# Memory attention and gated FFN on one core: tokens in five padded chunks, the first batch's keys loaded first, one summing group a batch

## The chip, the cores and the metric

The kernel runs on 1 core of a Trainium2 chip. The metric is the device time of one execution in microseconds (us). Three runs of the kernel before took 730.93 to 731.76 us, median 731.49.

## What is computed

```python
# q, k, v: (8, 8, 576, 64); phi: (8, 8, 576, 32); w_in: (512, 2048); w_out: (2048, 512); float32
a = softmax(phi, axis=2)                    # over the 576 tokens, for each memory
k_m = einsum('bhsm,bhsd->bhmd', a, k)       # 32 memory keys a head
v_m = einsum('bhsm,bhsd->bhmd', a, v)
attn = softmax(q @ k_m.T / 8, axis=-1)      # over the 32 memories
x = (attn @ v_m) laid out as (8 * 576, 512)
h = x @ w_in
out = (h * erf(log1p(exp(-abs(h))) + maximum(h, 0))) @ w_out
```

## The kernel before

The 8 batches follow each other. For each batch the kernel first makes the memories, folds the values into the first weight (vw = v_m times w_in, head by head), makes the attention weights `at`, and then runs the FFN in 16 steps k of 128 hidden columns: `ffn1` (L666) gives h for 576 tokens in two halves of 288, ACT and DVE make g out of it, and `ffn2` (L758) adds g times w_out to four PSUM tiles `pso` of 128 tokens each. The 64 tokens that are left over from 4 x 128 are collected in `rest`, two batches side by side, and multiplied later (`ffn2_rest`, `psr`). Float32 operands are mostly split into a high and a low float32r part, so that a product is three matmuls (hi hi, hi lo, lo hi); the first four FFN1 steps and the first sixteen FFN2 steps run in plain float32 ("exact"), because the splits aren't ready then.

The weights come as 64-bit words. `decode` (L423) turns one piece of 256 columns into float32: two ACT steps (L435, L439) and three DVE steps (L429, L443, L465). The first batch needs w_in piece by piece: `vw` for piece c, then FFN1 of steps 2c and 2c + 1.

The memories of a batch: `memories` (L485) loads phi twice. `phiT` has memories on partitions: there DVE takes the maximum over tokens, and ACT makes the exponential whose sum is the softmax's divisor (`prs`). `phi` has tokens on partitions, in four chunks of 128 rows and a last one of 64 (L393 to L402, two transfers); the maximum is turned to that layout with ACT (L495) and TensorE (L501), DVE adds it and ACT takes exp (L507 to L516). `one_memory` (L530) then sums keys and values of four heads over the tokens:

```python
for c, (s0, ln) in enumerate(SC):
    for j in range(4):
        h = 4 * g + j
        nc.tensor.matmul(
            out=get(ps)[M * j : M * (j + 1), 0, :],
            lhsT=get(a)[:ln, c, h * M : (h + 1) * M],
            rhs=get(("kv", b, h // 2))[:ln, c, :, h % 2, :],
```

Keys and values of a head stand side by side (128 columns), four heads write the four quarters of the partitions, and there are two such groups (g = 0, 1) a batch: 20 matmuls each, shown as 40 in the profile, since a float32 matmul is recorded as two. ACT scales the sums (L550, L552), TensorE turns them (L557), ACT copies them to `km` and `vm` (L570, L573). `attention` (L616) makes scores of q and km for one half of a batch's tokens (u = 2b and 2b + 1) and runs their softmax on DVE and ACT (L629 to L650).

The order on every engine is written by a planner when the kernel is built (`Plan.order`, L126 on): each operation has costs, a rank and reads and writes, buffers of a pool are taken in turn, and the planner gives each engine a fixed order. In the start it also puts filler matmuls (`fill`, L361: zeros times zeros, "idle") into gaps that it foresees on TensorE, so many as fit. The engines run their queues in order; all loads and stores are issued by SP in one queue.

Of the kernel before, what the change touches and what calls it, by code (L numbers as in the profile page):

```python
# [28 lines left out]
SCRATCH = 1024  # L29

# [39 lines left out]
class Plan:  # L70
# [5 lines left out]
    SWITCH = 92.0  # L76
    RELOAD = 100.0
# [160 lines left out]
def tile_memory_attention_then_erf_softplus_ffn(  # L238
# [13 lines left out]
    H = 2 * kv.shape[1]  # L252
# [13 lines left out]
    SC = [(c * P, min(P, S - c * P)) for c in range((S + P - 1) // P)]  # L266
    RAW = 4
# [10 lines left out]
        for n, b, kw in (  # L278
# [9 lines left out]
            ("ot", 2, {}),  # L288
# [6 lines left out]
    room.update({"g_hi": 3, "g_lo": 3, "raw": RAW, "ot": 2, "ps": 4, "sc": 2, "dk": 1, "phiT": 2})  # L295
    room.update({f"pso{d}": 1 for d in range(NT)})
    for n in ("pmx", "psm", "prs"):
# [10 lines left out]
        "ot": ("ot", [P, DM], F32),  # L308
# [18 lines left out]
    def mm(n, exact):  # L327
        return 2 * (2 * n / 2.4 + 2.5) if exact else n / 2.4 + 11.7
# [10 lines left out]
    zeros = const.tile([P, 512], BF16, name="zeros")  # L339
# [21 lines left out]
    def fill(n):  # L361
        if n and not idle:
            idle.append(pools["po"].tile([P, DM], F32, name="idle", tag="pso0"))
        for _ in range(n):
            nc.tensor.matmul(out=idle[0], lhsT=zeros[:, :P], rhs=zeros, start=True, stop=True)


    def load(rank, key, nbytes, emit):
        op(SP, 60, rank, [], [key], emit, nbytes=nbytes)

    def load_weight(rank, name, c):
# [14 lines left out]
        load(rank, key, P * 8192, emit)  # L386

    def load_phiT(rank, b, g):
        key = tile_("phiT", "phiT", b, g)
        load(rank, key, P * S * 4,  # L390
             lambda: nc.sync.dma_start(out=get(key), in_=phiT[b, g * P : (g + 1) * P, :]))

    def load_tokens(rank, key, src, n_bytes, view):  # L393
        n = S // P
        load(rank, (key, "whole"), S // P * P * n_bytes, lambda: nc.sync.dma_start(
            out=view()[:, :n], in_=src[: n * P].rearrange("(p c) e -> p c e", c=n)))
        load(rank + 0.001, (key, "last"), SC[-1][1] * n_bytes, lambda: nc.sync.dma_start(
            out=view()[: SC[-1][1], n], in_=src[n * P :]))

    def load_phi(rank, b):  # L400
        key = tile_("raw", "phi", b, shape=[P, len(SC), H * M], pool="raw")
        load_tokens(rank, key, phi[b], H * M * 4, lambda: get(key))  # L402

    def load_kv(rank, b, p, tag="raw"):
        key = tile_(tag, "kv", b, p, shape=[P, len(SC), 2, 2, D], pool=tag)
        load_tokens(rank, key, kv[b, p], 4 * D * 4,
                    lambda: get(key).rearrange("p c x h d -> p c (x h d)"))

    def load_q(rank, u, tag="raw"):
        key = tile_(tag, "q", u, shape=[P, NP_, U], pool=tag)  # L410
        b, hf = divmod(u, 2)
        load(rank, key, P * NP_ * U * 4, lambda: nc.sync.dma_start(
            out=get(key),
            in_=qT[b, :, hf * U : (hf + 1) * U].rearrange("(p r) s -> r p s", r=P)))
# [70 lines left out]
    def memories(rank, rank_2, b):  # L485
        a = ("phi", b)
        n, ln = S // P, SC[-1][1]
        bias = tile_("dk", "bias", b, shape=[P, NG, P], pool="att")
        for g in range(NG):
# [5 lines left out]
            op(ACT, 320, rank, [mx], [(bias, g)], lambda g=g, mx=mx: nc.scalar.activation(  # L495
                get(bias)[:, g], ident, AF.Identity, scale=0.0, bias=get(mx)))
        ps = tile_("ps", "psa", "max", b, shape=[P, H * M], pool="ps")

        def turn():
            for g in range(NG):  # L500
                nc.tensor.transpose(  # L501
                    out=get(ps)[:, g * P : (g + 1) * P], in_=get(bias)[:, g], identity=ident
                )

        op(PE, 2 * 108, rank, [bias], [ps], turn)
        op(DVE, on_dve(n * H * M), rank, [(a, "whole"), ps], [(a, "whole")],
           lambda: nc.vector.tensor_tensor(  # L507
               out=get(a)[:, :n], in0=get(a)[:, :n],
               in1=get(ps).unsqueeze(1).to_broadcast([P, n, H * M]), op=ALU.add))
        op(DVE, on_dve(H * M), rank, [(a, "last"), ps], [(a, "last")],  # L510
           lambda: nc.vector.tensor_tensor(
               out=get(a)[:ln, n], in0=get(a)[:ln, n], in1=get(ps)[:ln], op=ALU.add))
        op(ACT, on_act(n * H * M), rank, [(a, "whole")], [(a, "whole")],
           lambda: nc.scalar.activation(get(a)[:, :n], get(a)[:, :n], AF.Exp), kind="exp")
        op(ACT, on_act(H * M), rank, [(a, "last")], [(a, "last")],
           lambda: nc.scalar.activation(get(a)[:ln, n], get(a)[:ln, n], AF.Exp), kind="exp")  # L516
# [10 lines left out]
        for g in range(NG):  # L527
            one_memory(rank_2 + g * 0.01, b, g)

    def one_memory(rank, b, g):  # L530
        a, rs = ("phi", b), ("prs", b, g)
        ps = tile_("ps", "psa", "kmvm", b, g, shape=[P, 4, P], pool="ps")
        t = tile_("dk", "kvk", b, g, shape=[P, 3 * D], pool="att")
        ps_2 = tile_("ps", "psa", "turn", b, g, shape=[P, 4, P], pool="ps")

        def sums():
            for c, (s0, ln) in enumerate(SC):
                for j in range(4):
                    h = 4 * g + j
                    nc.tensor.matmul(  # L540
                        out=get(ps)[M * j : M * (j + 1), 0, :],
                        lhsT=get(a)[:ln, c, h * M : (h + 1) * M],
                        rhs=get(("kv", b, h // 2))[:ln, c, :, h % 2, :],
                        start=(c == 0),
                        stop=(c == len(SC) - 1),
                    )

        op(PE, len(SC) * 215, rank, [a] + [("kv", b, 2 * g + j) for j in range(2)], [ps], sums,
           kind="small", holds=[t])
        op(ACT, 300, rank, [ps, rs], [(t, 0)], lambda: nc.scalar.activation(  # L550
            get(t)[:, 0 : 2 * D], get(ps)[:, 0, :], AF.Identity, scale=get(rs)))
        op(ACT, 190, rank, [(t, 0)], [(t, 1)], lambda: nc.scalar.activation(  # L552
            get(t)[:, 2 * D : 3 * D], get(t)[:, 0:D], AF.Identity))

        def turn():
            for r in range(2):
                nc.tensor.transpose(  # L557
                    out=get(ps_2)[:, r, :], in_=get(t)[:, r * D : (r + 2) * D], identity=ident
                )

        op(PE, 2 * 108, rank, [t], [ps_2], turn)
        for par in range(2):
            rows = slice(par * D, (par + 1) * D)

            def view(which, rows=rows, par=par):
                v = get(ps_2).rearrange("p r (pr e m) -> p r pr e m", e=2, m=M)
                return v[rows, which, :, par, :]

            op(ACT, 145, rank, [ps_2], [(("km", b % 2), (g, par))],
               lambda rows=rows, par=par, view=view: nc.scalar.activation(  # L570
                   km[b % 2][rows, 2 * g : 2 * g + 2], view(par), AF.Identity, scale=SCALE))
# [375 lines left out]
```

## Time and profile before

| | before |
|---|---|
| median of three runs | 731.49 us (730.93 to 731.76) |
| the profiled execution | 729.75 us, of which the span from first to last instruction is 728.0 us |
| TensorE matmuls (PE) | 720.0 us busy, 99% of the span, 4816 recorded |
| VectorE (DVE) | 521.0 us, 72% |
| ScalarE (ACT) | 449.9 us, 62% |
| GpSimd (POOL) | 98.7 us, 14% |
| bytes moved | 64.75 MB, mean 89 GB/s |

The profile shows one execution. Its busy share of PE holds the filler matmuls, and matmuls overlap, so that the busy share alone doesn't tell where time can be gained; the timeline of PE does. In the rows a line number is that of the kernel, `out<-in` are the program's names, `x40` counts the instructions that a row merges, and a row of a timeline begins with start and length in us.

### The profile page before, as it was taken

How to read it: one execution, taken by the hardware profiler on the slowest of the kernel's cores; microseconds unless marked ns; L12 is line 12 of the kernel's file. 1: busy time of each engine (PE TensorE's matmuls, PEld its weight loads, DVE VectorE, ACT ScalarE, POOL GpSimd, SP SyncE). 2: the span in 40 equal slices, each digit the busy share in tenths (PEclk: the TensorE clock that was granted, in tenths of full speed). 3: DMA queues.
4: the chain of work that ended last, by engine and by line, in shares of the span. 5: the costliest groups of instructions: out<-in, count | busy, mean ns of one | idle time of the engine just before them, and what ended most of it. 6: DMA issues, size and time to landing. Idle time of an engine off the chain costs nothing.

```text
span 728.0 us, 12307 instructions
## 1 busy us (share of the span) xinstructions
PE 720.0 (99%) x4816; PEld 553.8 (76%) x4816; DVE 521.0 (72%) x963; ACT 449.9 (62%) x708; POOL 98.7 (14%) x246
## 2 busy tenths in 40 slices
PE   9999999999999999999999999999999999999997
PEld 4456555578887888888788887888878788888885
DVE  3899999689677685877755587777854587666631
ACT  5799999875747666594644556474754266454611
POOL 0011001120111111111111011111111111111110
PEclk9999999999999999999999999999999999999999
DMA  9996332421503115111310214211210100010002
GB/s 321 391 389 227 100 149 82 161 100 43 173 24 108 42 39 178 35 59 34 107 57 1 91 48 127 70 59 33 66 33 1 59 15 0 1 45 15 1 1 72
DMA packets 30393, 64.75 MB, mean 89 GB/s; under 512 B 2688, under 2 KB 13440, under 8 KB 29312
## 3 DMA queue, kind: packets, MB, share of 16 engines
q1 hardware_dynamic: 30336, 63.97, 26.1%
q8 instruction: 38, 0.62, 0.4%
q14 instruction: 19, 0.16, 0.1%
HBM read 54.53 MB, written 9.44 MB: 88 GB/s over the span
## 4 chain that ended last, share of the span: by engine, by line
PE 87%; DMA 6%; ACT 4%; DVE 1%; SPq 1%; issue 1%
PE pso L754 48%; PE psh L681 26%; PE psr L754 6%; PE psa L583 5%; DMA w<-w_in 4%; PE psa L540 2%; DMA kv<-kv 2%; ACT w L439 1%; ACT w L435 1%; ACT e L709 0%; ACT L709 0%; PE psa L557 0%; ACT e L704 0%; DVE w L443 0%; ACT vw_hi L354 0%
## 5 line engine op out<-in xcount | busy, mean ns | idle before, releaser
L754 PE MATMUL pso<-wo,g_hi 128*128 128x512 f32 x896 | 280.8, 395 | 0.0
L704 ACT ACTIVATE e<-h 128x576 f32<-128x576 f32 x128 | 88.0, 687 | 171.5 <-DVE h L696 170.9
L754 PEld LDWEIGHTS pso<-wo,g_hi 128*128 128x128 f32 x896 | 160.0, 188 | 31.8 <-issue 6.3
L754 PE MATMUL pso<-wo,g_lo 128*128 128x512 f32 x448 | 176.1, 393 | 0.0
L696 DVE COPY h<-psh 128x288 f32<-128x288 f32 x239 | 107.8, 452 | 42.8 <-PE psh L681 41.2
L681 PE MATMUL psh<-at_hi,vw_hi 128*128 128x288 f32 x496 | 113.7, 310 | 0.0
L681 PE MATMUL psh<-at_hi,vw_lo 128*128 128x288 f32 x496 | 106.0, 295 | 0.3 <-DVE vw_lo L356 0.3
L681 PE MATMUL psh<-at_lo,vw_hi 128*128 128x288 f32 x496 | 106.1, 295 | 0.0
L681 PEld LDWEIGHTS psh<-at_hi,vw_hi 128*128 128x128 f32 x496 | 84.5, 188 | 27.8 <-issue 8.2
L735 POOL CAST rest<-g_hi 128x64 fp32r<-128x64 f32 x112 | 51.1, 457 | 391.3 <-DVE g_hi L730 385.5
L728 DVE TENSOR_TENSOR e<-e,h 128x576 f32<-128x576 f32 x112 | 82.7, 751 | 26.5 <-ACT e L709 26.4
L754 PEld LDWEIGHTS pso<-wo,g_lo 128*128 128x128 f32 x448 | 84.1, 188 | 19.2
L730 DVE CAST g_hi<-e 128x576 fp32r<-128x576 f32 x112 | 50.7, 457 | 63.1 <-PE pso L754 51.1
L731 DVE TENSOR_TENSOR g_lo<-e,g_hi 128x576 fp32r<-128x576 f32 x112 | 86.3, 771 | 4.4
L709 ACT ACTIVATE e<-e 128x576 f32<-128x576 f32 x128 | 80.3, 675 | 0.4
L681 PEld LDWEIGHTS psh<-at_hi,vw_lo 128*128 128x128 f32 x496 | 79.8, 188 | 0.7 <-DVE vw_lo L356 0.5
L681 PEld LDWEIGHTS psh<-at_lo,vw_hi 128*128 128x128 f32 x496 | 79.1, 188 | 0.0
L735 POOL CAST rest<-g_lo 128x64 fp32r<-128x64 f32 x112 | 37.8, 338 | 110.8 <-DVE g_lo L731 103.7
L754 PE MATMUL pso<-w,g 128*128 128x512 f32 x112 | 52.5, 599 | 0.0
L754 PE MATMUL psr<-wo,rest 128*128 128x512 f32 x192 | 49.0, 390 | 0.0
L354 ACT ACTIVATE vw_hi<-psa 128x512 fp32r<-128x512 f32 (+1 forms) x68 | 34.9, 556 | 19.6 <-PE psa L583 19.5
L356 DVE TENSOR_TENSOR vw_lo<-psa,vw_hi 128x512 fp32r<-128x512 f32 (+1 forms) x68 | 42.0, 632 | 6.5 <-ACT vw_hi L354 6.3
(82 smaller groups left out, 716.0 us busy)
## 6 DMA issues: line engine op xcount, KB each, us to landing
kv<-kv SPq DMA_DIRECT2D x32, 512.0 KB, 4.2
q<-qT SPq DMA_DIRECT2D x16, 576.0 KB, 5.0
w<-w_in SPq DMA_DIRECT2D x8, 1024.0 KB, 11.6
w<-w_out SPq DMA_DIRECT2D x8, 1024.0 KB, 11.2
out<-ot SPq DMA_DIRECT2D x32, 256.0 KB, 2.0
phiT<-phiT SPq DMA_DIRECT2D x16, 288.0 KB, 2.9
phi<-phi SPq DMA_DIRECT2D x8, 512.0 KB, 5.7
kv<-kv SPq DMA_DIRECT2D x32, 64.0 KB, 4.2
```

The costliest lines, as they stand in the source:

```text
L354: lambda: nc.scalar.activation(get_hi(), get_src(), AF.Identity))
L356: lambda: nc.vector.tensor_tensor(out=get_lo(), in0=get_src(), in1=get_hi().bitcast(F32), op=ALU.subtract))
L583: nc.tensor.matmul(out=get(ps[par])[p * M : (p + 1) * M, :], lhsT=w()[rows, p, :], rhs=x()[rows, p, :], start=True, stop=True,)
L681: nc.tensor.matmul(out=get(ps), lhsT=x[:, g, k % 4 * P : (k % 4 + 1) * P], rhs=y[:, g, :], start=(n + g == 0), stop=(n == len(parts) - 1 a ...
L696: lambda: nc.vector.tensor_copy(out=keep(), in_=get(ps)),
L704: last[:] = [op(ACT, on_act(S), rank, [("h", i)], [e], lambda: nc.scalar.activation(get(e), get(("h", i)), AF.Softplus), kind="softplus", ...
L709: last[:] = [op(ACT, on_act(S), rank, [e], [e], lambda: nc.scalar.activation(get(e), get(e), AF.Erf), kind="erf", edge=edge, after=last)]
L728: op(DVE, on_dve(S), rank, [e, h], [e], lambda: nc.vector.tensor_tensor(out=get(e), in0=get(e), in1=get(h), op=ALU.mult))
L730: op(DVE, on_dve(S, 1), rank, [e], [hi], lambda: nc.vector.tensor_copy(out=get(hi), in_=get(e)))
L731: op(DVE, on_dve(S), rank, [e, hi], [lo], lambda: nc.vector.tensor_tensor(out=get(lo), in0=get(e), in1=get(hi).bitcast(F32), op=ALU.subtract))
L735: lambda x=x, y=y: nc.gpsimd.tensor_copy(out=rest[:, k, x, cols], in_=get(y)[:, NT * P :]))
L754: nc.tensor.matmul(out=o, lhsT=y, rhs=z, start=(start and n == 0), stop=(stop and n == len(parts) - 1))
```

## The change

- **Tokens in five chunks on padded partitions.** The host lays keys, values and phi out as five chunks of 116 rows (the last 112), each on 128 partitions with zeros behind. phi, and each of the four kv tiles, is one transfer of 640 KB (before 512 + 64 KB). No chunk has 64 rows or fewer.
- **Keys and values apart.** A kv tile holds keys or values of four heads, not both of two; a summing matmul has 64 columns and not 128.
- **The first batch.** Its `phi` isn't loaded. The exponentials of `phiT` are turned on TensorE in ten transposes and copied out of PSUM (`numbers_of`), four chunks at once on ACT and the last on DVE. The sums of all keys are one group, those of all values another. The transfers stand in another order (`FIRST`).
- **The other batches** have one summing group with all four kv tiles (80 matmuls), four transposes in one piece, and half as many copies to km and vm, each twice as wide. Batch 1's loads and memories are due four steps later (`o - 8`, not `o - 12`).
- **Rest.** In the first 16 steps POOL writes the high and the low part of the left-over columns itself; `rest_split` on ACT and DVE is gone.
- **Stores.** The pool `ot` is gone; a store's tile takes a buffer of `phiT`. The last batch's tiles are copied out by ACT alone, not half by DVE.
- `raw` has five buffers, not four; the planner's costs of changing between small and large matmuls, and of a wide float32r matmul, are raised a little; a filler reads 128 zeros four times, and not 512.

```diff
-    FIRST = ["phiT0", "phiT1", "phi", "kv0", "kv1", "in0", "kv2", "kv3", "q0", "q1", "in1", "out0"]
+    FIRST = ["phiT0", "phiT1", "k0", "k1", "q0", "in0", "v0", "v1", "q1", "in1", "out0"]
...
+    def load_kv(rank, b, x, g):
+        key = tile_("raw", "kv", b, x, g, shape=[P, NC, 4 * D], pool="raw")
+        load(rank, P * NC * 4 * D * 4, [key],
+             lambda: nc.sync.dma_start(out=get(key), in_=kv[b, x, g]))
...
+        if not b:
+            tile_("raw", *a, shape=[P, NC, H * M], pool="raw")
+            n = NC - 1
+            for g in range(NG):
+                numbers_of(rank, b, g, range(n), tile_("ps", "psa", "a", g, shape=[P, n, P], pool="ps"), 0)
+            last = tile_("ps", "psa", "a", NG, shape=[P, NG, P], pool="ps")
+            for g in range(NG):
+                numbers_of(rank, b, g, range(n, NC), last, g)
+        for turn_n, part in enumerate(parts):
+            one_memory(rank_2 + turn_n * 0.01, b, part)
+
+    def numbers_of(rank, b, g, cs, ps, at):
...
+        def turn():
+            for c in cs:
+                nc.tensor.transpose(
+                    out=get(ps)[:ln, at + c - cs[0], :], in_=get(t)[:, c * ROW : c * ROW + ln], identity=ident
+                )
...
         def sums():
-            for c, (s0, ln) in enumerate(SC):
-                for j in range(4):
-                    h = 4 * g + j
-                    nc.tensor.matmul(
-                        out=get(ps)[M * j : M * (j + 1), 0, :],
-                        lhsT=get(a)[:ln, c, h * M : (h + 1) * M],
-                        rhs=get(("kv", b, h // 2))[:ln, c, :, h % 2, :],
-                        start=(c == 0),
-                        stop=(c == len(SC) - 1),
-                    )
...
+            for n, g in enumerate(gs):
+                for y, x in enumerate(xs):
+                    for c, ln in enumerate(ROWS):
+                        for j in range(4):
+                            h = 4 * g + j
+                            nc.tensor.matmul(
+                                out=get(ps)[M * j : M * (j + 1), n, y * D : (y + 1) * D],
+                                lhsT=get(a)[:ln, c, h * M : (h + 1) * M],
+                                rhs=get(("kv", b, x, g))[:ln, c, j * D : (j + 1) * D],
+                                start=(c == 0),
+                                stop=(c == NC - 1),
+                            )
...
+            op(POOL, 400, rank, [t], part[:1], lambda: nc.gpsimd.tensor_copy(
+                out=rest[:, k, 0, cols], in_=get(t)[:, NT * P :]))
+            op(POOL, 400, rank, [t, part[0]], part[1:], lambda: nc.gpsimd.tensor_tensor(
+                out=rest[:, k, 1, cols], in0=get(t)[:, NT * P :],
+                in1=rest[:, k, 0, cols].bitcast(F32), op=ALU.subtract))
...
-        t = tile_("h" if final else "ot", "ot", *o)
-        halves = [(0, DM // 2, ACT), (DM // 2, DM, DVE)] if final else [(0, DM, ACT)]
...
+        t = tile_("h" if final else "phiT", "ot", *o)
+        op(ACT, on_act(DM, True), rank - 30, [o], [t],
+           lambda: nc.scalar.activation(get(t)[:, :DM], get(o), AF.Identity))
```

Since the planner orders the work, the diff doesn't show how instructions move. The first place is SP's queue at the start of the program. Before:

```order
L391 DMA phiT<-phiT 128x576 x2
L395 DMA phi<-phi 128x1024
L397 DMA phi<-phi 64x256
L395 DMA kv<-kv 128x1024
L397 DMA kv<-kv 64x256
...
L377 DMA w<-w_in 128x4x256
...
L412 DMA q<-qT 128x4x288 x2
L377 DMA w<-w_in 128x4x256
```

Now:

```order
L396 DMA phiT<-phiT 128x576 x2
L405 DMA kv<-kv 128x1280 x2
L410 DMA q<-qT 128x4x288
L382 DMA w<-w_in 128x4x256
L405 DMA kv<-kv 128x1280 x2
L410 DMA q<-qT 128x4x288
L382 DMA w<-w_in 128x4x256
L387 DMA w<-w_out 128x1024
```

The keys and one q now stand ahead of the first piece of w_in, and the values behind it; before, two of four kv pieces (left out above) stood behind it, and both q behind them.

The second place is PE's queue at the memories of a later batch, among FFN matmuls (`pso`, `psh`); `w_in, vm` is a vw block (the numbers are those of buffers), `kv, phi` the sums, `ident, kvk` the transposes of the sums. Before:

```order
L583 MATMUL psa<-w_in_103,vm_102 32x512 x8
L540 MATMUL psa<-kv,phi 32x128 x20
L681 MATMUL psh<-at_hi,vw_hi 128x288 x2
...
L557 MATMUL psa<-ident,kvk 128x128 x2
L754 MATMUL pso<-wo,g_hi 128x512 x2
L754 MATMUL pso<-wo,g_lo 128x512
L540 MATMUL psa<-kv,phi 32x128 x20
L754 MATMUL pso<-wo,g_hi 128x512 x2
```

Now:

```order
L617 MATMUL psa<-w_in_100,vm_99 32x512 x8
L566 MATMUL psa<-kv,phi 32x64 x80
L715 MATMUL psh<-at_hi,vw_hi 128x288 x2
...
L587 MATMUL psa<-ident,kvk 128x128 x4
L774 MATMUL pso<-wo,g_hi 128x512 x2
```

Two groups of 20, one of them alone among FFN matmuls, have become one of 80 behind a vw block. In batches 1 to 7 there were 14 such groups, 8 of them alone; now there are 7, one alone. The whole program has 78 fillers, and had 112.

## Rows read from the trace of the kernel before

**Rows 1.** The page, part 1: busy us (share of the span) xinstructions of each engine.
```profile
PE 720.0 (99%) x4816; PEld 553.8 (76%) x4816; DVE 521.0 (72%) x963; ACT 449.9 (62%) x708; POOL 98.7 (14%) x246
```

**Rows 2.** Windows: stretch, its length, each engine's busy us, PEclk, DMA share, GB/s.
```profile
0.00:48.70 48.70, 46.52 (x346) 23.62 (x347) 34.96 (x60) 34.14 (x62) 1.80 (x7) 1.00 1.00 363
48.70:130.00 81.30, 80.12 (x556) 46.63 (x554) 75.54 (x123) 78.06 (x126) 8.41 (x16) 1.00 0.46 158
```

**Rows 3.** Timeline of PE, 0 to 60 us; in brackets idle before it and releaser.
```profile
15.43 1.97 PE L540 MATMUL psa<-kv,phi 128*32 128x128 f32 x40
...
22.09 7.73 PE L365 MATMUL idle<-zeros 128*128 128x512 bf16 x35
29.66 4.04 PE L681 MATMUL psh<-at,vw_hi 128*128 128x288 f32 x16
...
38.08 0.66 PE L583 MATMUL psa<-w_in,vm 64*32 64x256 f32 x16
...
48.76 1.88 PE L754 MATMUL pso<-w,g 128*128 128x512 f32 x4
```

**Rows 4.** Chain of waits, 0 to 60 us: start, us, what.
```profile
14.30 13.64 DMA w<-w_in
...
28.01 10.14 DMA w<-w_in
```

**Rows 5.** Timeline of PE, pieces between 231 and 282 us.
```profile
231.56 0.71 PE L583 MATMUL psa<-q,km 64*32 64x288 f32 x16
232.20 0.73 PE L754 MATMUL pso<-wo,g_hi 128*128 128x512 f32 x2
...
270.18 1.09 PE L583 MATMUL psa<-w_in,vm 64*32 64x512 f32 x16
271.20 1.43 PE L540 MATMUL psa<-kv,phi 128*32 128x128 f32 x40
...
279.29 0.40 PE L754 MATMUL pso<-wo,g_lo 128*128 128x512 f32 x1
279.62 1.43 PE L540 MATMUL psa<-kv,phi 128*32 128x128 f32 x40
280.98 0.73 PE L754 MATMUL pso<-wo,g_hi 128*128 128x512 f32 x2
281.55 0.40 PE L754 MATMUL pso<-wo,g_lo 128*128 128x512 f32 x1
281.79 0.63 PE L754 MATMUL pso<-wo,g_hi 128*128 128x512 f32 x2
```

**Rows 6.** Line 540 (count: ns min/median/max, first and last start); windows of its instructions.
```profile
L540 PEld LDWEIGHTS psa<-kv,phi x640: 102/110/110, 9.6 to 529.0; 128*32 128x32 f32 x128, 64*32 64x32 f32 x32
L540 PE MATMUL psa<-kv,phi x640: 269/273/297, 9.6 to 529.1; 128*32 128x128 f32 x128, 64*32 64x128 f32 x32
279.62:279.65 0.03, 0.03 (x4) 0.03 (x5) 1.00 0.00 0
```

**Rows 7.** Waits of PE's weight loads, 120 to 140 us: total, times, longest.
```profile
PEld psa L540 <- DMA kv<-kv: 0.8, 1, 0.8
```

**Rows 8.** Timelines of ACT and DVE, 0 to 70 us.
```profile
5.59 0.76 ACT L521 ACTIVATE phiT<-phiT,pmx 128x576 f32<-128x576 f32 x1
...
13.00 1.16 ACT L435 ACTIVATE w<-w 128x1024 int32<-128x1024 uint32 x1
...
15.20 1.23 DVE L443 SCALAR_TENSOR_TENSOR w<-w 128x1024 int32<-128x1024 int32 x1 [1.68 <-ACT w L439]
...
21.87 1.37 DVE L632 TENSOR_REDUCE smx<-sc 128x18 f32<-128x576 f32 x2
```

**Rows 9.** Timelines of the last copies; last row: groups by form, busy us, mean ns.
```profile
723.37 0.42 DVE L803 COPY ot<-psr 128x256 f32<-128x256 f32 x1 [0.94 <-PE psr L754]
...
723.83 0.38 ACT L800 ACTIVATE ot<-psr 128x256 f32<-128x256 f32 x1 [0.98 <-DVE ot L803]
...
L800 ACT ACTIVATE ot<-psr 128x512 f32<-128x512 f32 x3 | 1.7, 581 | 0.0
```

More of the change, by code (lines that the diff above doesn't have):

```diff
@@ L265, in tile_memory_attention_then_erf_softplus_ffn @@
     REST = S - NT * P
-    SC = [(c * P, min(P, S - c * P)) for c in range((S + P - 1) // P)]
-    RAW = 4
+    NC = phi.shape[2]
+    ROWS = [min(ROW, S - c * ROW) for c in range(NC)]
+    assert NC == -(-S // ROW) and D < ROWS[-1]
+    RAW = 5
     HB, EB = 5, 5
@@ L364, in fill, with load @@
         for _ in range(n):
-            nc.tensor.matmul(out=idle[0], lhsT=zeros[:, :P], rhs=zeros, start=True, stop=True)
-    def load(rank, key, nbytes, emit):
-        op(SP, 60, rank, [], [key], emit, nbytes=nbytes)
+            nc.tensor.matmul(
+                out=idle[0].rearrange("p (n c) -> p n c", c=P), lhsT=zeros,
+                rhs=zeros.unsqueeze(1).to_broadcast([P, DM // P, P]), start=True, stop=True,
+            )
+    def load(rank, nbytes, keys, emit):
+        op(SP, 60, rank, [], keys, emit, nbytes=nbytes)
     def load_weight(rank, name, c):
@@ L384, in emit @@
                 )
-        load(rank, key, P * 8192, emit)
+        load(rank, P * 8192, [key], emit)
     def load_phiT(rank, b, g):
         key = tile_("phiT", "phiT", b, g)
-        load(rank, key, P * S * 4,
+        load(rank, P * S * 4, [key],
              lambda: nc.sync.dma_start(out=get(key), in_=phiT[b, g * P : (g + 1) * P, :]))
[L393 to L398, printed above, removed]
-    def load_phi(rank, b):
[L401 to L407, printed above, removed]
+    def load_phi(rank, b):
+        key = tile_("raw", "phi", b, shape=[P, NC, H * M], pool="raw")
+        load(rank, P * NC * H * M * 4, [key], lambda: nc.sync.dma_start(out=get(key), in_=phi[b]))
+    def load_kv(rank, b, x, g):
+        key = tile_("raw", "kv", b, x, g, shape=[P, NC, 4 * D], pool="raw")
+        load(rank, P * NC * 4 * D * 4, [key],
+             lambda: nc.sync.dma_start(out=get(key), in_=kv[b, x, g]))
     def load_q(rank, u, tag="raw"):
@@ L494, in memories @@
                 out=get(mx), in0=get(mx), scalar1=-1.0))
[L495 to L499, printed above, removed]
+        if b:
+            bias = tile_("dk", "bias", b, shape=[P, NG, P], pool="att")
             for g in range(NG):
-                nc.tensor.transpose(
-                    out=get(ps)[:, g * P : (g + 1) * P], in_=get(bias)[:, g], identity=ident
-                )
@@ L505, in memories @@
[L505 to L516, printed above, removed]
+                op(ACT, 320, rank, [("pmx", b, g)], [(bias, g)], lambda g=g: nc.scalar.activation(
+                    get(bias)[:, g], ident, AF.Identity, scale=0.0, bias=get(("pmx", b, g))))
@@ L517, in memories @@
+            op(ACT, on_act(NC * H * M), rank, [a], [a], lambda: nc.scalar.activation(
+                get(a)[:ROW], get(a)[:ROW], AF.Exp), kind="exp")
         for g in range(NG):
@@ new lines, in numbers_of, with turn, keep @@
+    def numbers_of(rank, b, g, cs, ps, at):
+        t, a, n, ln = ("phiT", b, g), ("phi", b), len(cs), ROWS[cs[0]]
+        def turn():
+            for c in cs:
+                nc.tensor.transpose(
+                    out=get(ps)[:ln, at + c - cs[0], :], in_=get(t)[:, c * ROW : c * ROW + ln], identity=ident
+                )
+        def keep(f):
+            return lambda: f(get(a)[:ln, cs[0] : cs[-1] + 1, g * P : (g + 1) * P],
+                             get(ps)[:ln, at : at + n])
+        op(PE, n * 108, rank, [t], [(ps, at)], turn)
+        op(DVE, on_dve(n * P), rank, [(ps, at)], [(a, (g, cs[0]))],
+           keep(lambda y, x: nc.vector.tensor_copy(out=y, in_=x)),
+           other={ACT: (on_act(n * P, True), keep(
+               lambda y, x: nc.scalar.activation(y, x, AF.Identity)))})
@@ L853, in tile_memory_attention_then_erf_softplus_ffn @@
             when(2 * c - 1, vw, at(2 * c - 1.5), 0, c, 1, 2 * c < FR1)
-        when(2 * c, decode, at(second[2 * c] - 3.5), "out", c)
+        when(2 * c, decode, at(second[2 * c] - 2.5), "out", c)
         n = second[16 + 2 * c] - 5 - c if 2 * c < FR2 else second[2 * c] - 2
```

151 lines of the change are left out of this document (72 added, 79 removed).

## The prediction

> **What bounds the kernel now.** I read the page's busy times first: TensorE (PE) is busy 99% of the span, and no other engine comes near that [rows 1]. That figure includes filler matmuls that compute nothing, so the second look is at two stretches [rows 2]: up to 48.7 us PE is busy 46.52 us at a granted clock of 1.00, and from 48.7 us on it is busy 80.12 of 81.30. The third look is PE's timeline of the first stretch [rows 3]: 35 fillers stand in one piece ahead of the first FFN1 matmul, which starts at 29.66, and the first FFN2 matmul starts at 48.76. So there are two regimes. Up to 48.76 PE waits for data: the chain of waits there runs over the transfers of w_in, which landed at 27.94 (14.30 + 13.64) and 38.15 (28.01 + 10.14), and over ACT that decodes them [rows 4]. After 48.76 PE is the bound, and whatever takes a PE slot is paid in full, whatever leaves one is gained in full. The change is therefore priced in three places: the start, the small matmuls inside the dense stream, and the end.
>
> **The small matmuls in the stream.** A block of summing matmuls that stands alone starts at 279.62, and the next FFN2 matmul starts at 280.98 [rows 5]: a body of 1.36 us. Standing alone it pays for the way in and out as well: from the last FFN2 start at 279.29 to 280.98 are 1.69, less the 0.24 of that matmul itself (281.55 to 281.79), and 0.10 more because the first two behind it take 0.73 where others take 0.63; 1.55 in all, so 0.19 for way in and out. Joined to a block of w_in or q it doesn't pay that again. The body has ten passes of four matmuls side by side (five chunks, two passes for float32). What a pass costs per column I take from two other blocks with the same number of matmuls and two passes: w_in with 512 columns takes 1.02 (270.18 to 271.20), q with 288 takes 0.64 (231.56 to 232.20) [rows 5]. That is 0.38 us for 224 columns twice, 0.85 ns a column and pass. So 128 columns are 0.109 us, ten passes 1.09, and 0.27 of the body is fixed; I put half of that (0.13) down to the last chunk, whose 64 rows use another shape of the array; the change has no such chunk.
>
> After the change one group has 80 matmuls of 64 columns: 40 passes of four. The columns streamed are the same, the weight loads and the instructions double. The pass of 64 columns is not in the trace. Lower bound: half of 0.109, 0.055 us. Upper bound: 0.109, if a pass can't be shorter than it is now, because each weight load is recorded with 110 ns [rows 6]. I take 0.056, near the lower end. The row that it is nearest to: the matmuls of a body last 273 ns in the median and 297 at most [rows 6], and I read the longest as those that had to wait for a weight load, so a load that nothing hides adds some 24 ns and fits behind 56. Four of the matmuls and five loads are also under way within 0.03 us [rows 6], so issuing them one by one isn't what spaces the passes.
>
> The Trainium skill (page "TensorE: Matmul & The Clock Gate", section "Wait — 56ns, not 53.3ns?") says that matmuls never start closer than about 25 ns, however few columns they have; by that, four would take 0.100 us and not 0.056, and the time would be an estimated 735.4 us, close to the second rival's. The trace disagrees inside a pass (four in 0.03 us) and leaves the mean over shorter passes open (now 1.09 us over 40 records, 27 ns each).
>
> The body after: 0.14 + 40 x 0.056 = 2.38 us. Before, batches 1 to 7 have 14 bodies of 1.36 and 8 of them stand alone: 19.0 + 8 x 0.19 = 20.6. After, 7 bodies, one alone: 16.7 + 0.2 = 16.9. The stream gains **3.7 us**; with 0.109 a pass it loses 11.1. The transposes behind the sums stay 28 (four in one piece instead of two pairs). Those of the biases of batch 1 now stand behind the first FFN2 matmul: 0.2 us back. One wait of 0.8 us for a transfer of kv, in the stretch from 120 to 140 us [rows 7], I let stand: the joined group needs all four kv tiles at once, so it may stay, go or grow.
>
> **The start.** The transfers run at 363 GB/s [rows 2]: a key tile of 640 KB takes 1.8 us, half a q 1.6, a weight 2.9. phiT comes first as before and is in at 4.4. Then the keys are in at 8.0, q of the first half at 9.6, w_in 0 at 12.5, the values at 16.1, the second q at 17.7, w_in 1 at 20.6, w_in 2 at 26.4 (before 27.94), w_in 3 at 32.2 (before 38.15, because batch 1's phi and kv stood ahead of it). Durations for the walk: exp of phiT 0.76, a decode step 1.16 on ACT and 1.23 on DVE, a softmax step of 576 elements 0.69 (two in 1.37) [rows 8]; a group that follows at once starts some 0.1 earlier than the end that is recorded.
> - phi's numbers: two exps from 5.3 (before 5.59 [rows 8], behind a step that is gone) to 6.8, ten transposes, two copies of 512 columns: ready at 8.2. Sums of the keys at 8.3 (before, the second half's waited until 15.43 [rows 3]), km complete at 11.0, scores of the first half at 11.1.
> - DVE: two transposes, then five softmax steps between the three decode steps of w_in 0: the first half's attention is ready at 21.3. The values' sums end at 17.5, vm at 19.3, the first vw at 20.6. First FFN1: 21.4, against 29.66.
> - Then DVE has four steps of the second half and three of w_in 1: ready at 28.2. The other exact FFN1 matmuls run from 28.3.
> - w_in 2 is decoded behind them (merge, at_lo, sign): its vw at 32.0, against 38.08 [rows 3].
> - ACT: two splits, the table, the softplus steps; FFN1 of step 4 at 36.2; w_in 3 decoded, vw at 40.8; the first FFN2 at 43.1, against 48.76.
>
> That is 5.7 us, and six more FFN1 matmuls of 0.13 us (0.8) stand ahead of that point than before: **6.4 us**. Upper bound: the program has 78 fillers for 112; 34 at 0.22 (35 in 7.73 [rows 3]) are 7.5, and some 1.0 of PE's idle time (48.70 less 46.52 less the first 1.19 us, in which nothing can start) could go too: 8.5. Lower bound: the walk has six hand-overs between in-order queues; half a microsecond lost at each leaves 3.4.
>
> **The end.** Before, a DVE copy (0.42 from 723.37) and an ACT copy (0.38 from 723.83) follow each other [rows 9]: 0.84. One ACT copy of 512 columns takes 0.58 [rows 9]. Gain **0.26**.
>
> **At nothing.** Splitting rest's columns moves from one ACT and one DVE step per eight k to a second POOL step per k: POOL is busy 14% [rows 1]; uncovered, it would make rest late, which is read only when two batches are through. The padding adds 2 MB to 65 MB of transfers, under matmuls. The 'ot' tiles now share two buffers with phiT; stores and loads of phiT lie a good batch apart, and if they collide, ACT's copies hold PSUM and PE waits some 0.6 us a batch. SP issues fewer transfers.
>
> **The sum.** 6.4 + 3.7 + 0.26 - 0.2 = 10.2 us. The profiled execution took 729.75 us (span 728.0, the rest lies around it), 1.74 below the median of 731.49; so 719.5 for a run like it and **721.3 us** against the median.
>
> **The rivals.**
> 1. The start gains little: DVE and ACT were already busy 35 of the first 48.7 us, and the order puts the second half's softmax behind the decode. If the first FFN2 starts at 46 and not 43.1: gain 3.5 + 3.7, so 724.2. For it: the in-order queues. Against it: the late w_in 3, which ended the chain before, comes 6 us earlier.
> 2. The passes don't get shorter (slower). Doubling weight loads and matmuls then doubles the body: at 0.109 a pass it is 4.50 and the stream loses 11.1; the two bodies on the start's path (20 passes each) take 1.06 longer each, so the start gains 4.3. Together 738.2. The point from which it decides: the stream is even at 0.069 a pass, the whole at about 0.090. For it: the recorded 110 ns of a load equal the pass of today. Against it: the 24 ns above.
> 3. The joined group waits: it needs four kv tiles and both halves of phi, and its transposes follow close behind. 0.6 us a batch over seven batches, 4 us: 725.5.
> 4. Passes partly cover the loads (0.080): body 3.34, stream loses 3.0, so 728.
>
> **How the numbers follow.** Forecast 0.66, rival 1 0.10, rival 2 0.10, rival 3 0.09, rival 4 0.05. The forecast's own bounds: start 8.5 and the wait for kv gone gives 718.4; start 3.4 gives 724.3. The range of 717.5 to 727 takes in the forecast and rivals 1 and 3, and leaves out 2 and 4. A measurement of this kernel can tell about 0.2% (1.5 us) from no change: faster 0.87, within 0.03, slower 0.10.
>
> **What would show it.** Right: first FFN1 near 21.4 and first FFN2 near 43; a summing group of 80 matmuls that takes near 2.4 us; PE at clock 1.00 and without gaps behind. Wrong: a group over 3.8 us, a first FFN2 past 46, new idle time of PE at the sums or at the stores, or a granted clock of 1.2 GHz in the start, where fewer fillers stand: there each exact FFN1 matmul would take twice its time.

## The result, and the profile after

The changed kernel took 725.52 us in the median of four runs (724.70 to 726.16), the kernel before 731.62 beside it (730.93 to 731.95). The ratio is 0.9917 with an interval of 0.990 to 0.9934: faster by 6.1 us where 10.2 were forecast. The time lies in the range of 717.5 to 727.0, 4.2 us above the forecast of 721.3.

The profiled execution after the change took 725.42 us, its span is 722.9 (before 729.75 and 728.0). First the page's part 1, then the windows of the two regimes, cut at the first FFN2 matmul of this kernel (45.48); they answer to [rows 1, 2].

```profile
PE 709.6 (98%) x5430; PEld 555.6 (77%) x5430; DVE 517.8 (72%) x950; ACT 434.1 (60%) x644; POOL 100.1 (14%) x262
```
```profile
0.00:45.48 45.48, 39.96 (x404) 22.00 (x405) 33.60 (x59) 31.52 (x53) 1.65 (x8) 1.00 0.98 373
45.48:130.00 84.52, 82.55 (x590) 49.61 (x589) 76.52 (x121) 76.35 (x112) 18.16 (x30) 1.00 0.42 149
```

PE is still the bound and its granted clock is 1.00. But in the second window it stands idle for 1.97 us (84.52 less 82.55), before for 1.18. PE's timeline of the start (it answers to [rows 3]; in brackets the idle time before a row and its releaser):

```profile
19.93 0.72 PE L617 MATMUL psa<-q,km 64*32 64x288 f32 x16 [0.70 <-DMA q<-qT]
...
23.71 2.18 PE L715 MATMUL psh<-at,vw_hi 128*128 128x288 f32 x8 [0.19 <-DVE at L684]
...
34.40 0.67 PE L617 MATMUL psa<-w_in,vm 64*32 64x256 f32 x16 [0.39 <-DVE w_in L463]
...
43.19 0.67 PE L617 MATMUL psa<-w_in,vm 64*32 64x256 f32 x16 [0.49 <-DVE w_in L463]
...
45.48 1.88 PE L774 MATMUL pso<-w,g 128*128 128x512 f32 x4
```

Every point of the walk comes 2.3 to 2.4 us later than forecast: first FFN1 23.71 (21.4), vw of w_in 2 at 34.40 (32.0), of w_in 3 at 43.19 (40.8), first FFN2 45.48 (43.1). Next, pieces of PE's timeline in the stream. The joined group (it answers to [rows 5]) is as forecast: 2.39 us from its start to the next. Two gaps are new:

```profile
267.16 1.09 PE L617 MATMUL psa<-w_in,vm 64*32 64x512 f32 x16
268.18 2.45 PE L566 MATMUL psa<-kv,phi 116*32 116x64 f32 x160
270.57 0.53 PE L715 MATMUL psh<-at_hi,vw_hi 128*128 128x288 f32 x2
...
82.06 2.45 PE L566 MATMUL psa<-kv,phi 116*32 116x64 f32 x160
...
90.10 0.84 PE L617 MATMUL psa<-q,km 64*32 64x288 f32 x16 [1.83 <-DMA q<-qT]
...
181.46 2.43 PE L566 MATMUL psa<-kv,phi 116*32 116x64 f32 x155
184.91 0.31 PE L566 MATMUL psa<-kv,phi 112*32 112x64 f32 x5 [1.01 <-issue]
```

At 90.10 the scores of batch 1 wait 1.83 us for their q. At 184.91 a summing group stops for 1.01 us with five records to go (called the hole from here on); "issue" is time in which PE waited for nothing that the profile shows. A third wait is gone, that of 0.8 us for kv [rows 7]: no wait of PE for kv is left behind the start.

Where the time went is read by cutting the span in three. The forecast in this form: 48.76 less 5.7; 674.57 less 3.7 and 0.8, plus 0.2; 4.64 less 0.26.

| us | first FFN2 at | from there to the end of the last matmul | rest | span |
|---|---|---|---|---|
| before | 48.76 | 674.57 | 4.64 | 728.0 |
| forecast | 43.1 | 670.3 | 4.4 | 717.8 |
| after | 45.48 | 672.94 | 4.44 | 722.9 |

So 2.4 us are missing in the start and 2.7 in the stream (called so from the first FFN2 matmul to the end of the last matmul). The end came as forecast (0.2 for 0.26). Outside the span lie 2.5 us in this execution and 1.75 in the one before; the forecast took this part as unchanged.

### The profile page after: what moved, and what is told of

Same layout as the page of the kernel before. It is cut to its first block, busy times and chain, and to the rows that moved or that the text cites. A ratio compares the mean times of both kernels' runs of the same rounds, so it can differ in the third digit from the quotient of the medians.

```text
span 722.9 us, 13383 instructions
## 1 busy us (share of the span) xinstructions
PE 709.6 (98%) x5430; PEld 555.6 (77%) x5430; DVE 517.8 (72%) x950; ACT 434.1 (60%) x644; POOL 100.1 (14%) x262
## 4 chain that ended last, share of the span: by engine, by line
PE 89%; ACT 6%; DMA 3%; SPq 1%; issue 1%; DVE 0%
PE pso L774 48%; PE psh L715 26%; PE psr L774 6%; PE psa L617 5%; DMA q<-qT 3%; PE psa L566 2%; ACT w L437 1%; ACT w L433 1%; ACT e L738 1%; SPq L405 1%; ACT e L743 1%; ACT L738 1%; ACT h L731 0%; PE idle L367 0%; PE psa L587 0%
## 5 line engine op out<-in xcount | busy, mean ns | idle before, releaser
L770 POOL CAST rest<-g_hi 128x64 fp32r<-128x64 f32 x112 | 44.6, 400 | 408.6 <-DVE g_hi L765 396.1
L770 POOL CAST rest<-g_lo 128x64 fp32r<-128x64 f32 x112 | 35.8, 320 | 91.9 <-DVE g_lo L766 91.1
```

Of the source, the lines that this page charges most:

```text
L770: lambda x=x, y=y: nc.gpsimd.tensor_copy(out=rest[:, k, x, cols], in_=get(y)[:, NT * P :]))
```

## The experiments

The time of a kernel is the median of its runs; landings and gaps are those of its one profiled execution. The trace counts 16 landing steps for each transfer. `EARLY` holds a group of the keys and a group of the values, `TOGETHER` one group of all four tiles. The theory behind the first runs: the forecast's mechanism holds; the start is late because transfers land late; the stream lost what the two new waits cost.

**The change once more** (no edit).

> The changed kernel once more, unaltered. Two oddities of its first profile are in question: in the first key tile the last of 16 landing steps came 1.7 us behind the others, and 1.0 us of idle time stood inside the group of 80 summing matmuls at 184 us. Theory (both belong to the program): both come again, first FFN1 within 0.5 us of 23.7, time 725.5 us, within 1. Rival (chance of one execution): the keys are complete near 8.0 instead of 8.8 and 10.4, first FFN1 near 22.0, no hole at 184; the time of that execution is then 2 to 3 us below 725.4.

724.57 us (ratio 0.9904, 0.9888 to 0.992). The hole is there again (0.98 us at 183.88), and so is the wait for q (1.81). The late landing is not fixed: the last step of the first key tile came at 7.27, not 8.83, and first FFN1 at 22.71. So the hole and the wait belong to the program, the size of the delay to the execution.

**Batch 1 in two groups.**

```diff
-        when(n, memories, at(n), at(n + 3), b, TOGETHER)
+        when(n, memories, at(n), at(n + 3), b, EARLY if b == 1 else TOGETHER)
```

> Batch 1 alone sums its keys and its values in two groups of 40; all else as in the change. Theory: PE's wait of 1.8 us at 88 us comes from the buffers of raw, which phi and four kv tiles hold until the one group of 80 is done, so that q of batch 1 is issued too late; with the keys summed first their two buffers come free earlier, q is issued earlier and the wait shrinks below 0.5 us. One more block in the stream costs about 0.2 (way in and out). Time 1.2 to 1.7 us below the change's. Rival: q is late because of the transfer of w_out that stands ahead of it in the queue, or because batch 1's memories are due late; then the wait stays above 1.2 us and the time is within 0.5 of the change's.

723.70 us (ratio 0.9897), and PE doesn't wait for q in batch 1 any more:

```profile
86.77 1.33 PE L566 MATMUL psa<-kv,phi 116*32 116x64 f32 x80
...
89.01 0.93 PE L617 MATMUL psa<-q,km 64*32 64x288 f32 x16
```

But my reason was not the right one. The issues of SP, first of the change, then of this kernel (start, length, line):

```profile
75.33 7.14 SPq L387 DMA_DIRECT2D w<-w_out  x2
82.89 0.94 SPq L410 DMA_DIRECT2D q<-qT  x2
84.61 0.34 SPq L400 DMA_DIRECT2D phi<-phi  x1
```
```profile
74.93 7.06 SPq L387 DMA_DIRECT2D w<-w_out  x2
82.50 0.94 SPq L410 DMA_DIRECT2D q<-qT  x2
88.19 0.34 SPq L400 DMA_DIRECT2D phi<-phi  x1
```

q is issued 0.39 us earlier, no more. It landed at 88.29 for 89.97, 5.79 us after its issue and not 7.08: its last landing step came 0.52 us behind its first, in the change 1.85. Batch 2's phi and kv now come 3.6 us later, which may be why, but that isn't shown: in the kernel with smaller packets (below) phi follows q as closely as in the change, and q took 5.72. Besides, 1.26 us of sums now stand between. In both kernels q stands behind a w_out in SP's queue, and its issue follows the first summing matmuls by 0.8 us: a buffer of raw comes free then. So q doesn't wait for the whole group, as the theory had it; it hangs on the first sums of batch 1, which stand late in PE's queue (with the later rank, below, at 71.56 and not 82.06), and on its landing. The hole stayed (1.6 us here), and the time fell by 0.9 to 1.8, less than single runs of the change differ (722.75 to 726.42).

**Two groups in every batch.**

```diff
-        when(n, memories, at(n), at(n + 3), b, TOGETHER)
+        when(n, memories, at(n), at(n + 3), b, EARLY)
```

> In every batch the keys and the values are summed in two groups of 40 (the columns stay 64). 41 blocks of small matmuls stand in the stream for 38. Theory: the gain of the stream is the shorter pass, not the joining, and the joined group brings waits of its own (1.8 us at 88 for q, 1.0 at 184 within the group). Then three more ways in and out cost 0.6, seven more fixed parts of 0.1 a body 0.7, and the two waits go (2.8): 1.0 to 2.0 us below the change. Rival: joining is what gained. Then seven more groups at 0.3 to 0.5 each cost 2 to 3.5 us, and waits of this size come at other places: 1 to 3.5 us above the change.

722.85 us (ratio 0.988, 0.9866 to 0.9894): 1.7 to 2.7 below the change, neither wait is left, and the stream takes 671.33. A body of 80 records takes 1.26 us:

```profile
265.71 1.33 PE L566 MATMUL psa<-kv,phi 116*32 116x64 f32 x80
266.97 0.53 PE L715 MATMUL psh<-at_hi,vw_hi 128*128 128x288 f32 x2
```

Two of them are 2.52, a joined group 2.39: joining saves 0.13 a batch and a way in and out where the second group stood alone. The joined groups cost 2.8 in waits.

**The chunk of 64 rows back.**

```diff
-ROW = 116
+ROW = 128
```

> Chunks of 128 rows and a last one of 64, as before the change; all else as in the change, the order on PE is the same. Each group of 80 has four chunks of 64 rows. Theory (the prediction's 0.13 us for a chunk of that shape): 28 of them in batches 1 to 7 cost 3.6 us, two on the start's path 0.3: 3 to 4.5 us above the change, and a group of 80 takes 2.8 us instead of 2.4. Rival: the shape costs nothing, a group takes 2.35 to 2.45 and the time is within 0.7 us of the change's.

728.69 us (ratio 0.9965), 3.2 to 4.1 above the change. A group takes 3.32 us, more than expected: 0.93 for four chunks, or 0.23 each.

```profile
269.47 3.39 PE L566 MATMUL psa<-kv,phi 128*32 128x64 f32 x160
272.79 0.53 PE L715 MATMUL psh<-at_hi,vw_hi 128*128 128x288 f32 x2
```

Seven groups make 6.5 us; the time rose less, because the scores of batch 1 waited 0.52 us and not 1.83 and the hole was 0.4 us. At this point I doubted the pass: with 0.23 for a chunk, two bodies of 1.36 without it would be 2.26, shorter than the 2.39 of the narrow group.

**128 columns again, from batch 1 on.** Keys and values of a head stand side by side in a tile (the host's order for batches 1 to 7 is changed to match).

```diff
+            for n, g in enumerate(gs if b else ()):
+                for c, ln in enumerate(ROWS):
+                    for j in range(4):
...
+                            out=get(ps)[M * j : M * (j + 1), n, :],
...
+                            rhs=get(("kv", b, j // 2, g))[:ln, c, j % 2 * 2 * D : (j % 2 + 1) * 2 * D],
```

> Batches 1 to 7 sum with 128 columns again (keys and values of a head side by side in a tile, 40 matmuls a group for 80), in one group and with five padded chunks; the order on PE is otherwise the change's. Theory: the narrow pass is no gain by itself; the body of the change (2.39 us for 160 records) is shorter than two bodies of before (1.37 each) because the chunk of 64 rows is gone (0.23 each in the run with 128 rows) and because the groups are joined (0.14). Then the wide group takes 2.1 to 2.2 us, and the time falls 1 to 2 us below the change's 725. Rival (the prediction's view: passes cost in proportion to columns, the chunk of 64 rows 0.13): a wide group takes 2.3 to 2.4 us and the time is within 0.6 of the change's.

My doubt fell: the group takes 2.33 us, as the prediction's view has it.

```profile
264.92 2.40 PE L565 MATMUL psa<-kv,phi 116*32 116x128 f32 x80
267.25 0.53 PE L726 MATMUL psh<-at_hi,vw_hi 128*128 128x288 f32 x2
```

So 64 columns cost 0.06 a group more than 128, and no more: a pass of 0.056 against half of a wide one. The time is 722.56 us (ratio 0.9875) all the same, 2.0 to 3.0 below the change and lower than either expectation. In the stream 2.1 us are saved: the hole at 180 us is gone (1.0), which no theory had foreseen, the wait for q is 1.44 and not 1.83, the wide passes save 0.4, and a smaller stop at 518 us (below) is gone too (0.3). The start of this execution came 1.7 us earlier:

```profile
22.03 2.18 PE L726 MATMUL psh<-at,vw_hi 128*128 128x288 f32 x8 [0.19 <-DVE at L695]
...
43.79 1.88 PE L785 MATMUL pso<-w,g 128*128 128x512 f32 x4
...
88.25 0.84 PE L628 MATMUL psa<-q,km 64*32 64x288 f32 x16 [1.44 <-DMA q<-qT]
```

**The chunk of 64 rows with 128 columns** (`ROW = 128` in that kernel).

> 128 columns a matmul and chunks of 128 rows with a last one of 64, groups joined. It measures the chunk of 64 rows in the wide form. Theory (the prediction's 0.13 us for such a chunk): two of them a group, 2.33 + 0.26 = 2.55 to 2.65 us for the body. Rival: the 0.23 that a chunk cost in the narrow form belongs to the shape, whatever the columns; then 2.75 to 2.85.

One run, 723.81 us. The group takes 2.73, between the two expectations:

```profile
266.07 2.80 PE L565 MATMUL psa<-kv,phi 128*32 128x128 f32 x80
268.80 0.53 PE L726 MATMUL psh<-at_hi,vw_hi 128*128 128x288 f32 x2
```

The version without the waits, below, has 40 wide records without such a chunk:

```profile
81.44 1.30 PE L565 MATMUL psa<-kv,phi 116*32 116x128 f32 x40
82.67 0.66 PE L628 MATMUL psa<-w_in,vm 64*32 64x256 f32 x16
```

That is 1.23 us, and the three kernels with such chunks fit one rule. A body of before (1.36) has the chunk at its end: 0.13 more than 1.23, the prediction's figure. In the wide group one chunk is at the end and one in the middle: 0.40, so 0.27 in the middle. In the narrow group one is at the end, three in the middle: 0.13 + 3 x 0.27 = 0.94, measured 0.93. So a change between chunks of 128 and of 64 rows costs 0.13 us each time, and a chunk in the middle needs two: 1, 3 and 7 changes cost 0.13, 0.40 and 0.93. The Trainium skill (page "TensorEngine Tiling (Array Packing)", section "Tiling Modes") says that a change of tiling mode drains TensorE and gives no time; the runs fit it, with 0.13 us a change.

**The first tiles in smaller packets.**

```diff
+        for i, cs in enumerate((slice(0, NC - 1), slice(NC - 1, NC))):
+            load(rank + 0.001 * i, P * (cs.stop - cs.start) * 4 * D * 4, [(key, i)],
+                 lambda cs=cs: nc.sync.dma_start(out=get(key)[:, cs], in_=kv[b, x, g][:, cs]))
```

> The four key and value tiles of batch 0 are loaded in two transfers each (chunks 1 to 4, 4096 bytes a row; chunk 5, 1024 bytes). Theory: the first tile is late because single packets of 5120 bytes took 0.6 to 1.7 us where most take 0.196, which none of the 4096-byte packets before the change did (0.35 at most); with packets of 4096 the steps of the first key tile lie within 0.6 us, the second is in near 8.2 instead of 10.4, and first FFN1 comes 1 to 2 us earlier (near 22). Rival: the delay belongs to the place (the first touch of the kv array, so early in the program), not to the size of a packet; then the last step of the first tile stays over 0.9 us behind the median and first FFN1 stays at 23 to 24.

The rival held. In the first tile's first transfer the last step came at 6.66, 1.2 us behind the median, and packets of 4096 and of 1024 bytes took 0.66 to 1.09 us. First FFN1 at 24.17, time 724.18 (ratio 0.9898).

**A later rank for the second half's attention.**

```diff
-        attention(at(-8), at(-7 + 2 * u), u)
+        attention(at(-8 + 2 * u), at(-7 + 2 * u), u)
```

> The second half's attention of batch 0 gets a later rank, so that its transposes on DVE stand behind the first half's last step but two. Theory: in five executions first FFN1 started 3.91 us after the second q had landed, within 0.01, though its data don't need it: DVE's queue ties it to that transfer. With the order changed the tie is gone, first FFN1 comes 0.5 to 1.5 us earlier against the second q's landing, while the first FFN2, which hangs on w_in 1 to 3 behind it, moves by less than 0.5; the time stays within 1 of the change's. Rival: the second q isn't the bound, the vw of w_in 0 is; then first FFN1 stays within 0.3 of that distance. Or all of the start hangs on that first matmul: then first FFN2 comes as much earlier, and the time falls by 1.

As the theory has it: first FFN1 started 3.13 us after the second q had landed (22.42 less 19.29) and not 3.91; the first FFN2 25.29 after it and not 25.68. The chain of waits of the change shows the tie; the transposes of the second half (L663) stand on DVE ahead of the first half's last two steps (L677, L684):

```profile
7.56 12.23 DMA q<-qT
19.93 0.82 PE psa L617 x16
20.74 0.83 DVE sc L663 x2
21.57 0.64 DVE sc L677
22.21 0.66 DVE smx L666
22.87 0.70 DVE at L684
23.71 2.18 PE psh L715 x8
```

The time, 723.34 us (ratio 0.9884), fell by 0.2 to 1.2 more than expected; the new order also put batch 1's first sums at 71.56 and issued its q at 74.41, and the wait for it didn't come (the hole did, 1.12). In this execution the first key tile was in at 5.94, earlier than in any other execution with padded tiles; the last step of a value tile fell 1.6 us behind the others only at 16.05, and the second q came late by that.

**phi of batch 0 loaded, not turned.**

```diff
-        if b:
+        if True:
...
-    FIRST = ["phiT0", "phiT1", "k0", "k1", "q0", "in0", "v0", "v1", "q1", "in1", "out0"]
+    FIRST = ["phiT0", "phiT1", "phi", "k0", "k1", "q0", "in0", "v0", "v1", "q1", "in1", "out0"]
```

> The phi of batch 0 is loaded again ahead of the keys and shifted, not turned on TensorE; keys first, padded tiles and one group a batch stay. Theory: the whole start follows the landing of transfers in one queue; 640 KB more ahead of the keys at 363 GB/s delay every later landing by 1.8 us, so first FFN1 and first FFN2 come 1.5 to 2.1 us later and the time rises by as much, if the delay of the first key tile (1 to 3 us, single slow packets) stays. Rival A: that delay belongs to the first transfer of this kind at that time; then phi takes it, and the sum is the same. Rival B: DVE's and ACT's queues bind the start, the transfers don't: first FFN2 moves by less than 0.7 us.

727.64 us (ratio 0.994). Compared with the change's own execution, whose first tile was as late (8.83; here 8.80, for phi), the second q lands 1.36 us later, first FFN1 comes 1.36 later (25.07) and first FFN2 1.32 (46.80): less than expected, and the same at all three points, so the start does follow the queue of transfers. phi took the late step, as rival A says. The time rose by 2.1 to 3.1, more than expected; part of it is a second stop of PE behind a summing group, 0.94 us, where the change has 0.28 (below):

```profile
515.95 2.45 PE L566 MATMUL psa<-kv,phi 116*32 116x64 f32 x160
518.33 0.40 PE L715 MATMUL psh<-at_hi,vw_hi 128*128 128x288 f32 x1
519.67 0.29 PE L715 MATMUL psh<-at_hi,vw_hi 128*128 128x288 f32 x1 [0.94 <-issue]
```

**The kernel before once more** (no edit).

> The kernel before once more. In seven of nine executions with padded tiles the last of 16 landing steps of the first transfer behind phiT was 1.2 to 3.1 us behind the median; in the profile of before it was 0.2. Theory: this happens to whatever is transferred between 4 and 6 us, from execution to execution; here too the last step can be over 1 us late (chance a half or more), and then first FFN1 comes later than 29.66. Rival: it belongs to the new transfers; here all steps up to 10 us lie within 0.6 us, and first FFN1 starts at 29.66 within 0.3.

One run, 732.26 us, and the theory held: phi's last step came at 6.90 for 5.79, its other steps began at 5.23. Two rows of PE's timeline, to be laid beside [rows 3]:

```profile
31.58 4.04 PE L681 MATMUL psh<-at,vw_hi 128*128 128x288 f32 x16
...
51.32 1.88 PE L754 MATMUL pso<-w,g 128*128 128x512 f32 x4
```

**Without the waits: 128 columns, batch 1 in two groups by heads.** On top of the kernel with 128 columns, the sums over heads 0 to 3 and 4 to 7 of batch 1 are apart, all else joined.

```diff
+    BY_HEADS = [tuple((g, x) for x in range(2)) for g in range(NG)]
-        when(n, memories, at(n), at(n + 3), b, TOGETHER)
+        when(n, memories, at(n), at(n + 3), b, BY_HEADS if b == 1 else TOGETHER)
```

> 128 columns a summing matmul in batches 1 to 7, and batch 1 in two groups by heads, so that two of its kv tiles come free earlier; all else as in the change. Theory: the hole of 1.0 to 1.6 us at 180 us belongs to 160 records in 2.4 us and stays away with 80; the wait of 1.4 to 1.8 for q in batch 1 falls below 0.6 as it did with two groups there; the wide group saves 0.06 a batch. Sum 1.0 + 1.2 + 0.4: 2.5 us below the change's 724.6 to 725.5, so 722 to 723, if the first tiles land as late as in most executions. Rival: the wait for q comes back at the second half's q or at the transfers of w_out; then it is no faster than the wide kernel without it, and the wait for q sums to over 1.5 us.

720.05 us, ratio 0.9846 (0.9831 to 0.986): the fastest, 4.5 to 5.5 below the change and 2 to 3 lower than expected. Its PE waits (total, times, longest; all rows over 0.2 us but one of 0.4 for phiT's exp) all lie in the start:

```profile
PE psa L628 <- DVE w_in L463: 1.0, 3, 0.5
PE idle L367 <- DVE zeros L348: 1.0, 1, 1.0
PE psa L628 <- DMA q<-qT: 0.7, 1, 0.7
PE psa L577 <- DMA kv<-kv: 0.5, 1, 0.5
```

The stream takes 669.24, 3.7 less than in the change: the wait 1.8, the hole 1.0, the wide passes 0.4, the smaller stop at 518 us (below) 0.3, and 0.2 that I can't assign. The start was 1.1 us earlier (first FFN2 at 44.41), where the first key tile was in at 7.70 and not 8.83.

**128 columns and the later rank.** The two edits shown above, together.

> 128 columns a summing matmul in batches 1 to 7 and the later rank for the second half's attention of batch 0, joined groups everywhere. Theory: the two add up: the hole at 180 us goes (1.1), the wide passes save 0.4, and the order that the later rank brings moves batch 1's sums to 71 us, where q's wait shrinks to 0.9; 721.5 to 722.5. Rival: the order of the later rank gives nothing of its own; 722.5 to 723.5, as the wide kernel alone.

720.92 us (ratio 0.9855, 0.9838 to 0.9873), lower than either expectation. No hole, and no wait for q behind the start.

## Why the prediction was right and wrong

**The stream's term: right, and for its reasons.** A group of 80 matmuls takes 2.39 us (2.38 forecast); a pass of 64 columns costs what its columns cost; the chunk of 64 rows cost a body 0.13; a joined group saves the other's fixed part. Rivals 2 and 4 are out. The doubling of weight loads is hidden: 160 records in 2.39 us are 15 ns each. The Trainium skill's floor of about 25 ns between matmuls (page "TensorE: Matmul & The Clock Gate", section "Wait — 56ns, not 53.3ns?") would make that an estimated 4.0 us; here the trace disagrees, for matmuls that lie side by side in four column groups.

**The step that failed in the stream: "One wait of 0.8 us for a transfer of kv ... I let stand", with no new wait beside it in the sum.** It went, and two came: 1.83 for q of batch 1 and 1.01 within the dense group. The prediction itself names "new idle time of PE at the sums" as a sign of being wrong. PE's idle time in the stream rose from 1.18 to 3.28 us, which is 2.1 of the 2.7 us that the stream lacks. The other 0.6 lie in its busy time, which fell from 673.39 to 669.66, by 3.7 and not 4.3; why is open. Rival 3 named the place (the joined group) and a near price (4 us), but not the mechanisms: a buffer that comes free late and a matmul stream that stops inside the group. That its 725.5 us is the measured time is chance: it meant seven waits of 0.6 us. Batch 1's due date of four steps later was listed in the change and priced nowhere. In the kernels that leave batch 1's order alone the scores waited 0.5 to 1.8 us and began 0.13 after q had landed; where its sums are parted or moved the wait is gone.

**The step that failed in the start: "Then the keys are in at 8.0".** The walk behind the landings is right within 0.7 us where they are on time (22.03 and 43.79 for 21.4 and 43.1). It took one rate for a transfer, but a transfer is in when the last of its 16 steps is. What that last step does between 5 and 9 us differs from execution to execution, and later transfers keep the delay (in the run with the later rank it arose only at 16 us):

| execution | last step of the first tile behind phiT (before: phi, else keys) | second q in | first FFN1 | first FFN2 |
|---|---|---|---|---|
| before | 5.79 | | 29.66 | 48.76 |
| before, once more | 6.90 | | 31.58 | 51.32 |
| 128 columns (the same start as the change) | 6.15 | 18.11 | 22.03 | 43.79 |
| the change, once more | 7.27 | 18.80 | 22.71 | 44.48 |
| the change | 8.83 | 19.79 | 23.71 | 45.48 |

With the earliest landing the change's start is at 22.03 and 43.79, near the forecast of 21.4 and 43.1. Paired by the first tile's last step, the start gained 5.0 us (48.76 to 43.79) or 6.8 (51.32 to 44.48), where 5.7 were forecast. The pairing is rough: there are two pairs, and in the second the kernel before lost 2.56 us up to the first FFN2 where phi was only 1.11 late. So the runs don't show the start's term to be mis-sized; the profile of before was an execution without the delay, and that of after one with much of it. The walk missed one thing, the second half's transposes ahead of the first half's last steps on DVE: 0.8 us at first FFN1, 0.4 at first FFN2. This is rival 1's reason, the in-order queues; its first FFN2 at 46 was nearly met (45.48), but mostly by late landings.

**What follows for the sum.** Against the profiled execution of before, the change lacks 5.1 us of the forecast within the span and 0.8 outside it. Against the medians it lacks only 4.2, because the profile of before was 1.74 us faster than its median and that of after 0.1; that the miss is 4.2 and not 5.9 is luck. A gain of the forecast's size could be reached, though with another order of batch 1: the version without the two waits takes 720.05, 11.7 below the runs of before beside it, 0.4 of it from the wide passes.

## What to carry to other kernels

Price a joined group not only by its own time, but by when the buffers that it reads come free and by what is queued behind them; where a later due date stands in a diff, follow the next tile of that pool through the DMA queue. Read the first microseconds of a kernel from more than one execution before a start is dated to a microsecond. Keep chunks of one array shape together, or pad them: every change between 128 and 64 rows cost 0.13 us here, and narrow passes cost next to nothing more, but one of the seven groups of 160 records had a hole of 1.0 to 1.6 us.

## What was not expected of the hardware

- A summing group of 160 records stopped for 0.98 to 1.6 us at the same place in all six executions where the group there is 160 records of padded chunks, and for 0.4 with chunks of 64 rows; never where it was 80 records (16 or 29 ns each). A fetch of 16 KB of instructions, 0.9 to 1.4 us long, starts near that place in every one of these kernels, those without a hole too, and in the change another starts at 437.62 within the group that begins at 436.28, which has no hole; so it alone isn't the cause, and what stops PE there is left open. No other group of 160 has a hole inside. But in the same six executions, and in no other, PE stops once more within 1.1 us behind the last of these groups (near 515 us), for 0.19 to 0.94 us: three times put down to "issue", three times to a step of DVE.
- Between 4 and 7 us single DMA packets took 0.6 to 1.7 us where most of their size took 0.2 or less; the first tile's last step was 0.2 to 3.0 us behind its median. The packets hit key tiles, phi, packets of 5120, 4096 and 1024 bytes, and not every execution (none over 0.6 us in the profile of before, the first with 128 columns, and the one with the later rank). Why is open. The Trainium skill (page "DMA: Bandwidth & Descriptors", section "Why a DMA increments its semaphore by 16 and not by 1") says that a transfer's engines finish independently and only the full count means that it is in; the 16 steps here agree: batch 1's scores began 0.13 us behind the last step of their q.
